# The first batch by halves of d with DMA transposes, and the seven-product form from the third chunk on

## The chip, the cores and the metric

One core of a Trainium2 chip runs the kernel. The metric is the device time of one execution in microseconds (us); lower is better.

## The reference

The input x has 8 batches of 3008 rows of 256 (f32). Each column d of a batch is convolved circularly with a filter, by a real FFT over the rows, a product with a complex filter, and the inverse FFT. The result goes through a two-layer MLP with 2048 hidden units and a leaky ReLU.

```python
X = np.fft.rfft(x, axis=1)
y = np.fft.irfft(X * (filt_r + 1j * filt_i)[None], n=x.shape[1], axis=1)
h = y.reshape(24064, 256) @ w_in          # w_in 256 x 2048
out = np.maximum(0.01 * h, h) @ w_out     # w_out 2048 x 256
```

## The kernel before

**The FFT.** 3008 = 94 x 32. A batch goes through four stages: s1 (matmuls with a 94-point DFT for each of 32 residues n), a transpose, s2 (32-point DFTs with twiddles, 24 groups of frequencies, then the product with the filter `fa_sb`), sa (the inverse 32-point DFTs), a second transpose, and sb (the inverse 94-point DFTs), whose results, 376 tokens for each of 8 groups h and each half dt of d, are copied to `yt`, the input of the MLP.

**The MLP** goes over 47 chunks of 512 tokens. `moe1` makes the hidden units of a chunk: 32 matmuls with 512 columns (L528) into two wide PSUM tiles, and eight leaky ReLUs on ACT (L531). The second layer of a chunk is done one chunk later. `plain` does it in 64 matmuls with 256 columns (L693). `products` does it in the Winograd form of Strassen's scheme: seven products of quarter matrices, 112 matmuls with 128 columns (L601), with four sums of the hidden units on VectorE (`act_sums`, L567) and sums of the results. Chunks with a number of at least `W0` = 3 take the second form. Its sums lie in `big0`.

**The order** of all instructions is written out. Every step is put on a heap with a time in units of which a chunk takes `SL` = 8, and issued in the order of these times; the numbers in `REST`, `PLANS`, `YD`, `AFTER`, `SUMS` and others are such times and delays. Batches 1 to 7 run their FFT between the chunks of the MLP. `REST` places six sb groups of batch 0 (`late_sb`) that are left over from the start.

**Batch 0** has a list of its own, `FIRST`: each word names a step, and each engine works through its own part in that order. `s1p`, `s2p`, `sap` and `sbp` are matmuls into one of the five banks b0 to b4; `s1e`, `sae`, `sbe` copy a bank to SBUF on ACT (A) or VectorE (D); `s2d` multiplies a bank with the filter on VectorE; `s2a` copies a bank to SBUF on ACT for `s2m` to multiply on GpSimd; `t1` and `t2` are VectorE's 32x32 transposes (L399, L445), four calls each; `x`, `w_out` issue loads; `xc` rounds the early part of x to f16; `warm` are matmuls without use; `blank` clears rows of `x_sb`. Steps with a first argument hf or dt work on a half of d.

**Loads.** SP's queue brings constants and the first `EARLY` = 6 of the 32 residues of x as f32 (L225). The rest of x, the tables f2 and i1, the filter (first the half hf = 0, then hf = 1) and the weights are cast to f16 by GpSimd's software queue (L207 to L238, L474). Batches 1 to 7 transpose with `dma_start_transpose` on SP after s1 (L277) and through DRAM after sa; batch 0 does not.

Of the kernel before, what the change touches and what calls it, by code (L numbers as in the profile page):

```python
# [78 lines left out]
def kernel(  # L79
# [210 lines left out]
    def paired(t):  # L290
        return t[:].rearrange("p (e n t) -> p n e t", n=Q, t=2)

    def spread(dst, n0, ps, copy, e0=0):
        nn, de = ps.shape[1], ps.shape[2] // 2
        copy(paired(dst)[:, ds(n0, nn), ds(e0, de)], ps.rearrange("p n (e t) -> p n e t", t=2))
# [528 lines left out]
```

## Time and profile before

| | |
|---|---|
| median of 3 runs | 740.85 us (740.0 to 741.22) |
| the profiled execution | 740.64 us, its span 738.8 us |
| TensorE, VectorE, ACT, GpSimd busy | 730.5, 508.7, 549.3, 168.0 us |
| TensorE's granted clock | 1.00 of full speed throughout |
| first matmul of the MLP (L528) | starts at 34.71 us |
| last matmul of the last product | ends at 734.85 us |

The span is what the profiler records of one execution; the execution's own time is somewhat longer. A line of a profile names the source line (L528), the engine (PE is TensorE, PEld its weight loads, DVE VectorE, ACT ScalarE, POOL GpSimd, SP SyncE; SPq, ACTq and POOLq their queues), the operation, the tiles it writes and reads, and how often; timelines begin with start and duration in us, and brackets give the engine's idle time before an instruction and what ended it.

### The profile page before, as it was taken

How to read it: one execution, taken by the hardware profiler on the slowest of the kernel's cores; microseconds unless marked ns; L12 is line 12 of the kernel's file. 1: busy time of each engine (PE TensorE's matmuls, PEld its weight loads, DVE VectorE, ACT ScalarE, POOL GpSimd, SP SyncE). 2: the span in 40 equal slices, each digit the busy share in tenths (PEclk: the TensorE clock that was granted, in tenths of full speed). 3: DMA queues.
4: the chain of work that ended last, by engine and by line, in shares of the span. 5: the costliest groups of instructions: out<-in, count | busy, mean ns of one | idle time of the engine just before them, and what ended most of it. 6: DMA issues, size and time to landing. Idle time of an engine off the chain costs nothing.

```text
span 738.8 us, 19530 instructions
## 1 busy us (share of the span) xinstructions
PE 730.5 (99%) x8129; PEld 521.8 (71%) x8129; DVE 508.7 (69%) x696; ACT 549.3 (74%) x763; POOL 168.0 (23%) x171
## 2 busy tenths in 40 slices
PE   8999999999999999999999999999999999999997
PEld 3666677777777777777777777777767777777776
DVE  7878557776677667676777668666767676465566
ACT  4775787887788778887688777888767777777762
POOL 5605411333221312212132322222031220000000
PEclk9999999999999999999999999999999999999999
DMA  9978778778755595556855477434863433112012
GB/s 203 228 109 171 189 150 170 178 172 167 188 134 126 138 193 143 130 145 126 183 131 137 122 157 169 115 90 110 149 172 95 117 106 94 55 55 66 29 46 71
DMA packets 128617, 98.44 MB, mean 133 GB/s; under 512 B 59296, under 2 KB 107296, under 8 KB 128336
## 3 DMA queue, kind: packets, MB, share of 16 engines
q1 hardware_dynamic: 112905, 79.37, 42.0%
q0 software_dynamic: 15056, 17.50, 15.7%
q8 instruction: 63, 1.03, 0.6%
q10 hardware_dynamic: 567, 0.32, 0.2%
q14 instruction: 26, 0.21, 0.1%
HBM read 45.97 MB, written 35.65 MB: 110 GB/s over the span
## 4 chain that ended last, share of the span: by engine, by line
PE 93%; SPq 2%; DMA 2%; DVE 1%; ACT 1%; POOL 0%; issue 0%; POOLq 0%
PE ph L528 42%; PE pf L601 18%; PE po_ps L601 18%; PE pf L269 2%; PE pf L362 2%; PE pf L315 2%; PE pf L337 2%; PE pf L693 1%; DMA x_sb<-in_x_dram 1%; PE po_ps L693 1%; SPq L277 1%; SPq L587 1%; DMA p_b_g<-p_b_g 1%; PE po_ps L384 0%; PE pf L436 0%; ACT yt L351 0%
## 5 line engine op out<-in xcount | busy, mean ns | idle before, releaser
L531 ACT ACTIVATE gt_c<-ph 128x1024 f16<-128x1024 f32 x376 | 385.4, 1025 | 132.3 <-PE ph L528 125.5
L528 PE MATMUL ph<-yt,w_in_sb 128*128 128x512 f16 x1504 | 447.3, 379 | 0.2 <-ACT yt L351 0.2
L601 PEld LDWEIGHTS <-gt_c 128*128 128x128 f16 x2800 | 201.8, 98 | 97.9 <-issue 1.3
L330 POOL TENSOR_TENSOR y_b_g<-p_b_g,p_b_g 128x512 f16<-128x512 f32 x84 | 118.1, 1407 | 421.1 <-DMA p_b_g<-p_b_g 288.1
L601 PEld LDWEIGHTS <-big 128*128 128x128 f16 x2128 | 151.4, 98 | 65.9
L528 PEld LDWEIGHTS <-w_in_sb 128*128 128x128 f16 x1504 | 117.7, 98 | 4.4 <-DVE yt L351 0.4
L324 DVE TENSOR_TENSOR p_b_g<-pf,fb_sb 128x512 f32<-128x512 f32 x78 | 53.7, 688 | 33.8 <-PE pf L315 20.3
L601 PE MATMUL po_ps<-wt_sb,gt_c 128*128 128x128 f16 x704 | 71.8, 219 | 0.0
L601 PE MATMUL pf<-wt_sb,gt_c 128*128 128x128 f16 x688 | 69.3, 219 | 0.0
L601 PE MATMUL pf<-wt_sb,big 128*128 128x128 f16 x704 | 68.7, 219 | 0.0
L601 PE MATMUL pf<-w_out_sb,gt_c 128*128 128x128 f16 x720 | 68.1, 219 | 0.0
L351 ACT CAST yt<-pf 128x376 f16<-128x376 f32 (+9 forms) x136 | 58.1, 441 | 12.2 <-PE pf L362 8.5
L601 PE MATMUL po_ps<-w_out_sb,gt_c 128*128 128x128 f16 x688 | 65.7, 219 | 0.0
L601 PE MATMUL po_ps<-wt_sb,big 128*128 128x128 f16 x688 | 65.5, 219 | 0.0
L567 DVE TENSOR_TENSOR gt_c<-gt_c 128x2048 f16<-128x2048 f16 x43 | 56.9, 1322 | 1.0
L327 DVE TENSOR_TENSOR p_b_g<-pf,fa_sb 128x512 f32<-128x512 f32 x84 | 57.2, 681 | 0.2
L567 DVE TENSOR_TENSOR big<-gt_c,big 128x2048 f16<-128x2048 f16 (+1 forms) x45 | 56.4, 1254 | 0.0
L567 DVE TENSOR_TENSOR big<-big,gt_c 128x2048 f16<-128x2048 f16 (+1 forms) x45 | 56.3, 1252 | 0.1
L567 DVE TENSOR_TENSOR big<-gt_c 128x2048 f16<-128x2048 f16 (+1 forms) x46 | 56.3, 1224 | 0.0
L339 ACT CAST big<-pf 128x512 f16<-128x512 f32 x84 | 49.0, 584 | 9.3 <-PE pf L337 7.4
L270 ACT CAST big<-pf 128x384 f16<-128x384 f32 x90 | 43.0, 479 | 11.5 <-PE pf L269 8.2
L362 PE MATMUL pf<-i_sb,big 128*128 128x94 f16 x448 | 37.0, 206 | 0.0
(98 smaller groups left out, 644.7 us busy)
## 6 DMA issues: line engine op xcount, KB each, us to landing
p_b_g<-p_b_g SPq DMA_DIRECT2D x156, 128.0 KB
out_dram<-ost_c_h SPq DMA_DIRECT2D x118, 128.0 KB
dz<-big SPq DMA_DIRECT2D x42, 256.0 KB
big<-dz SPq DMA_DIRECT2D x56, 192.0 KB
x_sb<-in_x_dram POOLq DMA_DIRECT2D x40, 192.0 KB, 4.2
x_sb<-in_x_dram POOLq DMA_DIRECT2D x2, 768.0 KB, 9.2
w_in_sb<-in_moe_w_in_dram POOLq DMA_DIRECT2D x1, 1024.0 KB, 13.1
w_out_sb<-in_moe_w_out_dram POOLq DMA_DIRECT2D x1, 1024.0 KB, 14.3
```

The source lines that it names most:

```text
L269: nc.tensor.matmul(ps[:, j, :], x_sb[:, 4 * h + j, ts(dt, P)], fwd1m[:, :NW], start=True, stop=True)
L270: copy(turn_in[:, :, dt, :, ds(4 * h, 4)], ps.rearrange("p n (q k) -> p k q n", q=4))
L324: nc.vector.tensor_tensor(p2[:], ps, fb, AL.mult)
L327: nc.vector.tensor_tensor(p1[:], ps, fa, AL.mult)
L330: ("y", b, g), lambda: nc.gpsimd.tensor_tensor(y1[:], p1[:], p3[:], AL.add)))
L339: nc.scalar.copy(st2[h % 3][:, ds(2 * (g % 2), 2), :], ps)
L351: copy(yt[:, dt, ds(to, 4 * n)].rearrange("p (a c) -> p a c", c=4), v[:, ds(a, n)])
L362: nc.tensor.matmul(ps[:, j, :], z2[h % 3][:, j, ts(dt, P)], i1_sb[:, 4 * h + j, :N1], start=True, stop=True)
L528: nc.tensor.matmul(ph[:, j, :], w_in_sb[:, dt, ts(ct, P)], yt[:, dt, ds(ci * CH % RING, CH)], start=(dt == 0), stop=(dt == NDT - 1))
L531: nc.scalar.activation(gts[ci][:, ds(2 * g, 2), :], ph, AF.Lrelu)
L567: nc.vector.tensor_tensor(*(v[:, ds(c0, n)] for v in (o, i0, i1)), op)
L601: nc.tensor.matmul(of[t], a()[:, c, ts(t, P)], w[:, c, :], start=(c == 0), stop=(c == NCH - 1))
```

## The change

In batch 0 the two halves of d go separate ways. The first half keeps VectorE's transposes after s1 (two calls), and its second transpose is done by four DMA transposes on SP (`turn2`); for that, its sa uses the products as weights. The second half takes x as weights in s1 and is transposed by three DMA transposes on SP (`turn1`), and keeps VectorE's second transposes (two calls). `FIRST` is a new list. Four more sb groups of batch 0 (first half of d, h = 4 to 7) leave it and are placed by `REST0` between the chunks. `EARLY` is 8, the rest of x comes in three loads of 8, `w_in` is loaded in two halves, and the first half of batch 1's x is issued earlier on GpSimd's queue. `W0` is 2, so that chunk 2 takes the seven-product form. The last stores of the last chunk use other queues, and many places and delays have new values.

```diff
@@ -99,29 +99,30 @@
     SL = 8
     NCH = NCT // 2
     QT = 4 * N1
-    W0 = 3
+    W0 = 2
     GAP = 0.6
     EXG = 0
     LANDED = 2.836
-    READ = 1.712
-    TURN = 0.889
-    TURNED = 2.3
-    TURNS = 1.015
-    MARGIN = 3.838
-    YD = (0.966, 1.75, 0.753, 0.432, 1.2)
-    SUMS_FIRST = (0.018, 2.103, 2.35, 4)
-    SUMS = (0.322, 1.569, 2.418, 4)
-    REST = (5.339, 14.69, 8.396, 11.015, 24.419, 20.72)
-    DUE = (3.52, 0.66)
+    READ = 1.863
+    TURN = 0.994
+    TURNED = 2.064
+    TURNS = 0.968
+    MARGIN = 3.703
+    YD = (0.966, 1.75, 0.753, 0.418, 1.2)
+    SUMS_FIRST = (0.01, 1.144, 2.226, 3.62)
+    SUMS = (0.322, 1.519, 2.723, 4)
+    REST = (5.723, 13.479, 13.889, 13.394, 25.953, 17.309)
+    REST0 = (0.946, 2.627, 7.4, 12.589)
+    DUE = (3.521, 0.66)
     TWICE = (2.2, 2.35)
     LEAD = (3.9, 7.293)
-    AFTER = (0.454, 0.757, 1.245, 2.615, 0.39, 0.731)
+    AFTER = (0.01, 0.757, 1.503, 2.615, 0.676, 0.653)
     PLANS = (
-        (0.01, 0.254, 12.6, 1.065, 4.3, 35.584, 2.78, 8.122, 1.518),
-        (23.983, 0.737, 42.87, 2.58, 7.4, 85.174, 2.85, 2.756, 2.12),
-        (47.4, 1.5, 77.28, 3.57, 5.62, 130.659, 2.547, 1.5, 1.552),
+        (0.141, 0.279, 12.6, 1.096, 4.948, 35.584, 2.78, 8.122, 1.518),
+        (23.983, 0.737, 42.87, 2.58, 7.4, 85.174, 3.091, 2.756, 2.12),
+        (47.008, 1.164, 77.28, 3.57, 5.62, 132.135, 2.547, 1.5, 1.552),
         (81.42, 2.0, 119.86, 3.87, 6.302, 177.538, 2.92, 1.5, 2.55),
     )
@@ -219,12 +220,12 @@
-    EARLY = 6
+    EARLY = 8
     x_early = big[1][:].bitcast(FP32)[:, : EARLY * D].rearrange("p (n d) -> p n d", n=EARLY)
     nc.sync.dma_start(small_sb[:, 0], small_d.ap()[:, 0])
     nc.sync.dma_start(x_early[:R1], bass.AP(tensor=x.tensor, offset=x.offset, ap=[[N2 * D, R1], [D, EARLY], [1, D]]))
     nc.sync.dma_start(small_sb[:, 1:], small_d.ap()[:, 1:])
-    for n0, nn in ((6, 10), (16, 10), (26, 6)):
+    for n0, nn in ((8, 8), (16, 8), (24, 8)):
         x_load(0, n0, nn)
     for i in range(2):
         nc.gpsimd.dma_start(f2_sb[:, ts(i, NC // FP), :], f2_d.ap()[i])
@@ -235,14 +236,22 @@
         if hf == 0:
             nc.gpsimd.dma_start(f2_sb[:, ts(2, NC // FP), :], f2_d.ap()[2])
     nc.gpsimd.dma_start(i1_sb[:], i1_d.ap())
-    nc.gpsimd.dma_start(w_in_sb[:], moe_w_in.rearrange("(dt p) c -> p dt c", p=P))
     nc.vector.memset(idle, 0.0)
...
-    nc.vector.memset(big[2][:].rearrange("p (e n t) -> p e n t", n=Q, t=2)[:, :, NC:Q, :], 0.0)
+    half = [t[:, ts(i, HALF)] for t in big for i in range(2)]
+    in0, in1, mid0, mid1, in2, in3 = half
+    mid1, in1 = (v[:, : NC * P] for v in (mid1, in1))
+    in1 = in1.rearrange("p (k q n) -> p k q n", k=NC, q=4)
+    mid1 = mid1.rearrange("p (k d) -> p k d", k=NC)
+    in2q = in2.rearrange("p (n q k) -> p n q k", n=N2, q=4)
+    out2 = in0.rearrange("p (n d) -> p n d", n=N2)
+    nc.vector.memset(big[1][R1:P, HALF + NC * P :], 0.0)
+    nc.vector.memset(in2q[:, :, :, NC:Q], 0.0)
+    nc.vector.memset(in3.rearrange("p (e n t) -> p e n t", n=Q, t=2)[:, :, NC:Q, :], 0.0)
     K4 = 4 * NC
...
@@ -384,33 +384,49 @@
             nc.tensor.matmul(po_ps.rearrange("p a d -> p (a d)"), idle[:, 0:P], idle,
                              start=True, stop=True)
-    def s1p(_, n0, n, b):
-        ps = fill(("s1", n0), b, n, D)
-        for j in range(0, n, 2):
-            nc.tensor.matmul(ps[:, ds(j, 2), :], fwd1[:N1], x_sb[:N1, ds(n0 + j, 2), :],
-                             start=True, stop=True)
-
-    def s1e(_, n0, n, e):
-        spread(big[0], n0, held.pop(("s1", n0)), engine[e])
+    def s1p(t, n0, b):
+        if t == 0:
+            ps = fill(("s1", t, n0), b, 4, DH)
+            nc.tensor.matmul(ps, fwd1[:N1], x_sb[:N1, ds(n0, 4), :DH], start=True, stop=True)
+            return
+        ps = fill(("s1", t, n0), b, 4, NW)
+        for j in range(4):
+            nc.tensor.matmul(ps[:, j, :], x_sb[:N1, n0 + j, DH:], fwd1m[:N1, :NW], start=True, stop=True)
+
+    def s1e(t, n0, e):
+        ps = held.pop(("s1", t, n0))
+        if t == 0:
+            engine[e](paired(in0)[:, ds(n0, 4)], ps.rearrange("p n (e t) -> p n e t", t=2))
+        else:
+            engine[e](in1[:, :, :, ds(n0, 4)], ps.rearrange("p n (q k) -> p k q n", q=4))
     def t1(i):
-        a = big[0][:].bitcast(FP32)[:, ts(i, E4 * Q)].rearrange("p (e n r) -> p e n r", n=Q // 2, r=2)
-        o = big[1][:].bitcast(FP32).rearrange("p (n e r) -> p e n r", n=Q // 2, r=2)
+        a = in0.bitcast(FP32)[:, ts(i, E4 * Q)].rearrange("p (e n r) -> p e n r", n=Q // 2, r=2)
+        o = mid0.bitcast(FP32).rearrange("p (n e r) -> p e n r", n=Q // 2, r=2)
         nc.vector.transpose(o[:, ts(i, E4)], a)
+    def turn1(c, n):
+        nc.sync.dma_start_transpose(mid1[:, ds(c, n)], in1[:, ds(c, n)].rearrange("p k q n -> p (k q n)"))
+
+    def turn2(h, n):
+        nc.sync.dma_start_transpose(out2[:, ds(h, n)], in2q[:, ds(h, n)].rearrange("p n q k -> p (n q k)"))
+
     def s2p(hf, c, n, i, b):
         ps = fill(("s2", hf, c, i), b, n, DH)
-        src = big[1][:].rearrange("p (n e r t) -> p n r e t", n=Q // 2, r=2, t=2)
+        src = mid0.rearrange("p (n e r t) -> p n r e t", n=Q // 2, r=2, t=2)
         for j in range(n):
-            v = src[:, (c + j) // 2, (c + j) % 2, ts(hf, DH // 2)]
+            v = mid1[:, c + j] if hf else src[:, (c + j) // 2, (c + j) % 2]
+            o = ps[:, j, :] if hf else ps[:, j, :].rearrange("p (e t) -> p e t", t=2)
             if i == 0:
-                nc.tensor.matmul(ps[:, j, :].rearrange("p (e t) -> p e t", t=2), f2_sb[:, c + j, :], v,
-                                 start=True, stop=True)
+                nc.tensor.matmul(o, f2_sb[:, c + j, :], v, start=True, stop=True)
                 continue
             for h in range(2):
-                nc.tensor.matmul(ps[ts(h, 64), j, :].rearrange("p (e t) -> p e t", t=2),
-                                 f2_sb[:, c + j, ts(1 - h, 64)], v, start=True, stop=True)
+                nc.tensor.matmul(o[ts(h, 64)], f2_sb[:, c + j, ts(1 - h, 64)], v, start=True, stop=True)
+
+    def load_w_in(i):
+        half = moe_w_in.shape[1] // 2
+        nc.gpsimd.dma_start(w_in_sb[:, :, ts(i, half)], moe_w_in.rearrange("(dt p) c -> p dt c", p=P)[:, :, ts(i, half)])
     def times_filter(eng, hf, c, n, i, x):
         eng.tensor_tensor(prods[hf][:, i, ds(c, n), :], x, fa_sb[:, ds(c, n), ts(hf, DH)], AL.mult)
@@ -432,25 +448,36 @@
     def sap(hf, c, b):
         ps = fill(("sa", hf, c), b, 4, DH)
+        if hf == 0:
+            for j in range(4):
+                for i, m in enumerate((inv2r, inv2i)):
+                    nc.tensor.matmul(ps[:, j, :], prods[0][:, i, c + j, :], m, start=(i == 0), stop=(i == 1))
+            return
         for i, m in enumerate((inv2r, inv2i)):
             nc.tensor.matmul(ps, m, prods[hf][:, i, ds(c, 4), :], start=(i == 0), stop=(i == 1))
     def sae(hf, c, e):
-        engine[e](paired(big[2])[:, ds(c, 4), ts(hf, DH // 2)],
-                  held.pop(("sa", hf, c)).rearrange("p n (t e) -> p n e t", t=2))
+        ps = held.pop(("sa", hf, c))
+        if hf == 0:
+            engine[e](in2q[:, :, :, ds(c, 4)].rearrange("p n q k -> p q n k"), ps.rearrange("p k (q n) -> p q n k", q=4))
+        else:
+            engine[e](paired(in3)[:, ds(c, 4)], ps.rearrange("p n (t e) -> p n e t", t=2))
     def t2(i):
-        a = big[2][:].bitcast(FP32)[:, ts(i, E4 * Q)].rearrange("p (e n r) -> p e n r", n=Q // 2, r=2)
-        o = big[0][:].bitcast(FP32).rearrange("p (h n e r) -> p h e n r", h=2, n=Q // 2, r=2)
-        nc.vector.transpose(o[:, i // 2, ts(i % 2, E4)], a)
+        a = in3.bitcast(FP32)[:, ts(i, E4 * Q)].rearrange("p (e n r) -> p e n r", n=Q // 2, r=2)
+        o = half[1].bitcast(FP32).rearrange("p (n e r) -> p e n r", n=Q // 2, r=2)
+        nc.vector.transpose(o[:, ts(i, E4)], a)
     def sb_matmuls(ps, dt, h):
         assert ("i1t",) not in issued
-        src = big[0][:].rearrange("p (h n e r t) -> p h n r t e", h=2, n=Q // 2, r=2, t=2)
+        src = half[1].rearrange("p (n e r t) -> p n r t e", n=Q // 2, r=2, t=2)
         for j in range(4):
             n2 = 4 * h + j
+            if dt == 0:
+                nc.tensor.matmul(ps[:, j, :], out2[:, n2], i1_sb[:, n2, :N1], start=True, stop=True)
+                continue
             for t in range(2):
-                nc.tensor.matmul(ps[64 * t : 64 * t + 64, j, :], src[:, dt, n2 // 2, n2 % 2, t, :],
+                nc.tensor.matmul(ps[64 * t : 64 * t + 64, j, :], src[:, n2 // 2, n2 % 2, t, :],
                                  i1_sb[:, n2, :N1], start=True, stop=True)
     def sbp(dt, h, b):
@@ -480,26 +507,26 @@
         nc.vector.memset(x_sb[R1:P, ts(i, N2 // 4), :], 0.0)
     FIRST = """
-        blank 0, blank 1, blank 2, xc 0 4 A, xc 4 2 D, blank 3, warm 18, s1p 0 0 4 b3, s1p 0 4 2 b0, warm 3, s1p 0 14 2 b1, s1e 0 4 2 D,
-        s1e 0 0 4 A, s1p 0 10 4 b4, s1e 0 10 4 A, s1p 0 6 4 b3, s1e 0 14 2 D, warm 4, s1p 0 20 4 b4,
-        s1e 0 6 4 D, s1p 0 16 4 b3, s1e 0 16 4 A, s1p 0 26 2 b2, s1p 0 24 2 b0, s1e 0 24 2 A, s1e 0 20 4 D,
-        s1p 0 28 2 b1, s1p 0 30 2 b4, s1e 0 26 2 D, s1e 0 30 2 A, s1e 0 28 2 D, t1 0, t1 1, warm 14,
-        s2p 0 0 4 0 b3, s2p 0 0 4 1 b2, warm 2, s2p 0 8 4 1 b0, s2a 0 0 4 0, s2a 0 0 4 1, t1 3,
-        s2p 0 12 4 1 b4, t1 2, s2d 0 8 4 1, s2p 0 12 4 0 b1, s2p 0 16 8 0 b3, s2m 0 0 4 0, s2m 0 0 4 1,
-        s2d 0 16 8 0, s2a 0 12 4 1, s2p 0 8 4 0 b2, s2p 1 16 8 0 b4, s2p 0 4 4 1 b0, s2a 0 12 4 0, s2d 0 8 4 0,
-        s2a 1 16 8 0, s2p 0 4 4 0 b1, s2p 1 16 8 1 b3, s2d 0 4 4 0, s2a 1 20 8 0, sap 0 8 b2, s2d 0 4 4 1,
-        s2a 1 16 8 1, s2a 1 20 8 1, s2m 0 12 4 0, s2p 0 16 8 1 b4, sap 0 0 b1, s2p 1 0 8 1 b3, s2m 0 12 4 1,
-        sap 0 12 b0, s2m 1 20 8 0, sae 0 8 A, s2d 0 16 8 1, sae 0 0 A, s2p 1 8 8 1 b4, sap 0 4 b2, s2d 1 0 8 1,
-        sap 0 16 b1, sae 0 12 A, s2p 1 8 8 0 b3, sap 0 20 b0, s2d 1 8 8 1, s2m 1 20 8 1, sae 0 4 A,
-        s2d 1 8 8 0, s2p 1 0 8 0 b4, sae 0 16 A, sap 1 20 b2, s2d 1 0 8 0, sap 1 12 b1, sae 0 20 A, sap 1 8 b0,
-        x 0, s2m 1 16 8 0, sae 1 20 A, s2m 1 16 8 1, x 1, w_out, sae 1 12 A, sae 1 8 A, sap 1 16 b3,
-        sae 1 16 A, sap 1 4 b2, t2 1, sae 1 4 A, sap 1 0 b4, t2 0, sae 1 0 A, warm 4, sbp 0 1 b1, sbp 0 4 b0,
-        sbp 0 0 b3, sbp 0 3 b2, t2 3, sbe 0 1 A, sbe 0 4 A, sbe 0 0 A, sbp 0 2 b4, sbp 0 7 b1, sbp 0 6 b0,
-        t2 2, sbe 0 2 A, sbe 0 7 A, sbp 0 5 b3, sbp 1 0 b4, sbp 1 1 b1, sbe 0 6 A, sbe 0 5 A, sbe 1 1 A,
-        sbe 0 3 D, sbe 1 0 D
+        blank 2, warm 14, blank 3, s1p 0 8 b2, blank 0, xc 4 4 D, blank 1, s1p 0 4 b4, xc 0 4 A, s1p 0 0 b3,
+        s1p 1 0 b0, s1e 0 4 A, s1p 1 4 b1, s1e 1 0 D, s1e 0 0 A, s1e 1 4 A, s1p 0 20 b4, s1p 1 8 b0, s1e 1 8 A,
+        s1p 0 12 b3, s1e 0 8 D, s1p 1 12 b1, s1p 0 16 b0, s1e 0 12 D, s1e 1 12 A, s1p 1 20 b1, s1p 0 28 b3,
+        w_in 0, s1e 0 16 A, s1p 0 24 b2, s1e 1 20 A, s1e 0 24 A, s1e 0 20 D, s1e 0 28 D, t1 1, s1p 1 16 b1,
+        s1p 1 24 b4, s1p 1 28 b2, warm 6, s1e 1 16 A, t1 0, s2p 0 0 8 0 b3, s1e 1 24 A, s1e 1 28 A,
+        s2p 0 0 8 1 b4, turn1 16 8, turn1 0 8, s2p 0 16 4 1 b1, s2p 0 16 4 0 b0, s2a 0 16 4 0, s2d 0 0 8 0,
+        s2a 0 16 4 1, s2p 0 8 8 0 b3, x 0, s2p 0 20 4 0 b2, s2d 0 0 8 1, s2p 0 20 4 1 b0, s2d 0 8 8 0,
+        s2a 0 20 4 0, s2p 0 8 8 1 b4, s2m 0 16 4 0, s2a 0 20 4 1, sap 0 0 b1, sap 0 4 b2, s2p 1 16 4 0 b0,
+        sae 0 0 A, s2d 0 8 8 1, s2p 1 0 8 0 b3, sap 0 8 b1, sae 0 4 A, s2p 1 0 8 1 b4, s2m 0 20 4 0,
+        s2a 1 16 4 0, s2d 1 0 8 0, turn1 8 8, s2p 1 16 4 1 b0, s2d 1 0 8 1, sae 0 8 A, s2m 0 16 4 1,
+        sap 0 12 b2, sap 0 16 b1, s2m 1 16 4 0, s2a 1 16 4 1, s2m 0 20 4 1, sae 0 12 A, s2p 1 8 8 0 b3,
+        sap 0 20 b2, sae 0 16 D, w_in 1, sae 0 20 A, s2d 1 8 8 0, s2p 1 20 4 0 b0, s2m 1 16 4 1, s2p 1 8 8 1 b4,
+        s2a 1 20 4 0, s2p 1 20 4 1 b1, sap 1 0 b2, s2d 1 8 8 1, sap 1 16 b3, sae 1 0 A, sap 1 4 b0, turn2 0 8,
+        sae 1 4 A, turn2 8 8, sap 1 12 b4, turn2 16 8, sap 1 8 b2, s2m 1 20 4 0, s2d 1 20 4 1, x 1, sae 1 12 A,
+        sae 1 16 D, sap 1 20 b1, turn2 24 8, sbp 0 0 b3, sae 1 8 D, sae 1 20 A, t2 1, sbe 0 0 A, warm 2, t2 0,
+        w_out, sbp 0 1 b3, sbe 0 1 D, sbp 0 2 b0, sbe 0 2 D, sbp 0 3 b2, sbp 1 0 b4, sbp 1 1 b1, sbe 0 3 A,
+        sbe 1 0 D, sbe 1 1 A
     """
-    steps = dict(s1p=s1p, s1e=s1e, t1=t1, s2p=s2p, s2d=s2d, s2a=s2a, s2m=s2m, sap=sap, sae=sae, t2=t2,
-                 sbp=sbp, sbe=sbe, x=load_x, w_out=load_w_out, xc=round_x, warm=keep_warm, blank=blank)
+    steps = dict(s1p=s1p, s1e=s1e, t1=t1, turn1=turn1, turn2=turn2, s2p=s2p, s2d=s2d, s2a=s2a, s2m=s2m, sap=sap, sae=sae, t2=t2,
+                 sbp=sbp, sbe=sbe, x=load_x, w_out=load_w_out, xc=round_x, w_in=load_w_in, warm=keep_warm, blank=blank)
     for step in FIRST.split(","):
         what, *args = step.split()
         steps[what](*(int(v) if v.isdigit() else v for v in args))
@@ -674,13 +701,13 @@  (last_three)
-            soon(0.02, lambda: (nc.sync, nc.scalar)[t].dma_start(*parts[0]))
+            soon(0.02, lambda: (nc.scalar, nc.sync)[t].dma_start(*parts[0]))
...
-            soon(0.02, lambda: store(ci, 2 + t, low[:, t, 1], P, P, queue=(nc.sync, nc.scalar)[t]))
+            soon(0.02, lambda: store(ci, 2 + t, low[:, t, 1], P, P, queue=nc.scalar))
@@ -702,6 +729,8 @@
     groups, first_use = [], {}
     for g in range(10, 16):
         at(REST[g - 10], lambda g=g: late_sb(1, g - 8, (act, dve)[g < 12 and g % 2]))
+    for h in range(4, 8):
+        at(REST0[h - 4], lambda h=h: late_sb(0, h, act))
     def plan(b, s1, s1_step, s2, s2_step, lag, sb, sb_step, xl, x_step):
         for g in range(16):
```

More of the change, by code (lines that the diff above doesn't have):

```diff
@@ L290, in paired @@
     def paired(t):
[L291 to L295, printed above, removed]
+        return t.rearrange("p (e n t) -> p n e t", n=Q, t=2)
     E4 = D // 2 // 4
-    def first_t1(i):
-        a = big[0][:].bitcast(FP32)[:, ts(i, E4 * Q)].rearrange("p (e n r) -> p e n r", n=Q // 2, r=2)
-        o = big[1][:].bitcast(FP32).rearrange("p (n e r) -> p e n r", n=Q // 2, r=2)
-        nc.vector.transpose(o[:, ts(i, E4)], a)
     ys = {}
@@ L396, in t1 @@
+    def s1e(t, n0, e):
[4 more added lines that the diff above has]
+            engine[e](in1[:, :, :, ds(n0, 4)], ps.rearrange("p n (q k) -> p k q n", q=4))
     def t1(i):
-        a = big[0][:].bitcast(FP32)[:, ts(i, E4 * Q)].rearrange("p (e n r) -> p e n r", n=Q // 2, r=2)
-        o = big[1][:].bitcast(FP32).rearrange("p (n e r) -> p e n r", n=Q // 2, r=2)
+        a = in0.bitcast(FP32)[:, ts(i, E4 * Q)].rearrange("p (e n r) -> p e n r", n=Q // 2, r=2)
+        o = mid0.bitcast(FP32).rearrange("p (n e r) -> p e n r", n=Q // 2, r=2)
```

## The prediction

> **What bounds the kernel now.** I read the page first, then the chain that ended last, the timeline of the first 45 us, the DMA tables of that stretch, and the waits of TensorE after it. The page and the chain say that TensorE sets the time once the MLP has started:
>
> ```profile
> PE 730.5 (99%) x8129; PEld 521.8 (71%) x8129; DVE 508.7 (69%) x696; ACT 549.3 (74%) x763; POOL 168.0 (23%) x171
> PE 93%; SPq 2%; DMA 2%; DVE 1%; ACT 1%; POOL 0%; issue 0%; POOLq 0%
> ```
>
> From the first L528 at 34.71 us to the last product at 734.85 the only wait of TensorE above 0.5 us that the waits give is one in batch 7, where a y block comes late:
>
> ```profile
> PE pf L337 <- POOL y_b_g L330: 1.2, 1, 1.2
> ```
>
> So the time is: when L528 can start, plus TensorE's dense work, plus few stalls, plus the tail (734.85 to 738.8). The change touches all four, the first most. The timeline of the start:
>
> ```profile
> 14.23 4.62 DVE L399 STREAM_TRANSPOSE big<-big 128x1024 f32<-128x1024 f32 x4
> 18.40 4.51 POOL L416 TENSOR_TENSOR prod<-spare,fa_sb 128x512 f16<-128x512 f32 x4 [0.25 <-DMA fa_sb<-in_filt_i_dram]
> 18.78 0.65 DVE L416 TENSOR_TENSOR prod<-pf,fa_sb 128x512 f16<-128x512 f32 x1
> 23.42 2.30 POOL L416 TENSOR_TENSOR prod<-spare,fa_sb 128x512 f16<-128x512 f32 x2 [0.50 <-DMA fa_sb<-in_filt_i_dram]
> 29.03 4.71 DVE L445 STREAM_TRANSPOSE big<-big 128x1024 f32<-128x1024 f32 x4
> 34.35 0.55 DVE L351 CAST yt<-ph 128x376 f16<-128x376 f32 x1 [0.17 <-ACT yt L351]
> 34.71 0.75 PE L528 MATMUL ph<-yt,w_in_sb 128*128 128x512 f16 x2 [0.22 <-ACT yt L351]
> ```
>
> Two things are to be seen. VectorE works almost without a gap from 18.78 to 34.90 (products with the filter, transposes, one copy), and the second L528 needs that copy. And the filter lands late: GpSimd waits for its first half until 18.38 (I call this F0) and for its second half until 23.40 (F1). Without L399's last two calls VectorE could not have multiplied before 18.38.
>
> The software queue that brings the filter is full there. Share of the 16 DMA engines (second last column; above 1 where packets overlap) and GB/s:
>
> ```profile
> 14.00:16.00 2.00, 2.00 (x11) 0.88 (x9) 1.85 (x3) 0.20 (x1) 1.26 (x3) 1.00 1.82 180
> 18.00:20.00 2.00, 1.65 (x33) 1.38 (x34) 1.44 (x3) 1.28 (x3) 1.75 (x3) 1.00 1.78 178
> 20.00:22.00 2.00, 2.00 (x40) 1.57 (x37) 2.00 (x3) 1.07 (x2) 2.00 (x3) 1.00 1.84 212
> ```
>
> **The change, part by part.** Terms are against the profiled execution (740.64 us, span 738.8), which lies 0.2 below the median of 740.85.
>
> *First half of d.* Two transposes instead of four stand before the first product with the filter. The last x lands at 12.31; one copy on ACT and one on DVE (0.66 each) follow, then two transposes of 1.16: VectorE is ready near 16.2 and TensorE's first s2p near 16.8 (16.71 now). But s2d needs F0. So VectorE idles until F0, and the 2.3 us that L399 gives up buy at most 18.78 - 18.38 = 0.4.
>
> *VectorE after F0.* In the new list it has four s2d of the first half, 4 x 1.22 = 4.9; then, needing F1, four s2d of the second half (4.9), one of 512 (0.68), three sae (3 x 0.66 = 2.0), two t2 (2.35) and three sbe (3 x 0.54 = 1.6): 11.5. Sum 16.4, against 16.1 now. The two transposes that go are given back as sae, as an sbe and a larger share of s2d. The end of the start is max(F0 + 4.9, F1) + 11.5; with the old F0 and F1 that is 23.4 + 11.5 = 34.9, just today's 34.90. Hence no gain, and each us by which F1 slips is a us lost.
>
> *What moves F1.* (1) Eight rows of x instead of six come as f32 by SP's queue. Both queues together move 223 GB/s into SBUF (below), so the 0.197 MB more of f32 cost 0.88 and the 0.098 MB less in the software queue save 0.44: +0.44 on all that follows; -0.44 if SP's queue were free.
>
> ```profile
> 4.00:6.00 2.00, 2.00 (x7) 0.77 (x6) 1.40 (x2) 0.00 (x0) 2.00 (x4) 1.00 1.06 223
> ```
>
> (2) Three DMA transposes (turn1) wait on SP for ACT's last s1e, near 15.1 to 15.9, and are issued back to back, 1.3 each as at L277. There they first move bytes 1.3 us after the issue began and move 128x1024 f16 (262 KB) at about 215 GB/s with the engines' share at 1, so 1.2 us of all engines:
>
> ```profile
> 48.96 1.36 SPq L277 DMA_TRANSPOSE big<-big  x1
> q1 hardware_dynamic: 595, 0.15, 37.0%
> ```
>
> (The second line is the DMA table from 48.9 to 51.0.) Thus 3.6 us of transposes begin at 16.4 to 17.2, before F0 and F1. What part of it delays the filter? A load of 192 KB of x beside one or two of them landed in 4.7 and 4.4 us instead of 4.2 and 4.3: 0.2 to 0.4 of 1.2 to 2.4, a part of 0.1 to 0.3. But that queue was nearly empty; two full queues (4 to 6 us) divided one rate, a part of 1. The nearest row in kind is the x load, in fullness the other; I take 0.4: 3.6 x 0.4 = +1.4, bounds +0.4 and +3.6.
>
> F1 = 23.4 + 0.44 + 1.4 = 25.3, and the start ends at 36.8: **+1.9** (bounds -0.4 and +4.1).
>
> The Trainium skill, "DMA: Bandwidth & Descriptors", section "Issuing engines are not separate DMA queues", says that DMAs of SP, ACT and GpSimd run on the same 16 engines and interleave, which speaks against this change; the 4 to 6 us row agrees. The same page ("DMA_TRANSPOSE effective BW") gives 261 GB/s, an estimate of 1.0 us for one transpose; by it the +1.9 would be +1.7.
>
> *Queues passed.* On GpSimd x 0 now stands before the first s2m: its issue (0.6) waits for a free slot. Today each software DMA issue from the ninth on waits for the landing of the one eight before, so x 0, the 17th, waits for F0 itself; s2m starts at F0 + 0.8. GpSimd then has 7 x 1.16 + issues, done before VectorE's sae 1 8: hidden. Half of w_in moves behind x 0, and x 1 and w_out keep their order. Today w_out lands at 43.4 and is first used at 45.30: 1.9 slack. With 7 transposes at the part 0.4 it lands 3.8 later, and the use is 1.9 + 1.2 (below) later: hidden, by 1.2; at part 1 it is not (rival). turn2 is hidden behind t2 if it lands by then; sbe 0 2 before sbe 1 0 is where it would show.
>
> *Four groups of the first d half (sb, h 4 to 7)* leave the start and come in chunks 0 and 1. On TensorE each is 4 matmuls of 94 columns, 0.17 (the L362 entries of the chain): +0.68. Three fall in chunk 0, where ACT is the bound: between 34.7 and 46 it is busy 10.6 of 11.3 us. Three more copies of 0.47 make +1.4, TensorE's 0.5 within it. I take **+1.2**, bounds +0.7 and +1.6.
>
> *Chunk 2 by seven products.* Plain: 64 matmuls at 0.109 = 6.98. Seven products: 112 at 0.0557 = 6.23.
>
> ```profile
> 49.02 0.44 PE po_ps L693 x4
> 727.64 0.89 PE po_ps L601 x16
> ```
>
> **-0.75**. VectorE's four sums (1.25 each) and larger adds come when batch 1's second stage has ended (place 24.7 of a 24 to 32 slot): hidden; without that cover up to +2.
>
> *Tail.* Today the last store waits on ACT's queue from 735.16 to 735.85 behind a 1.45 us issue. That one goes to SP, and ACT gets two issues of 0.6 instead: **-0.3** (0 to -0.4).
>
> *Places anew.* The wait of 1.2 in batch 7 arises where y's DMA stands behind transposes and stores on SP. Its order shifts by tenths of a slot, so it may go, stay or double: **-0.4** (-1.2 to +1).
>
> Sum: 1.9 + 1.2 - 0.75 - 0.3 - 0.4 = +1.65: profiled 742.3, median about 742.5.
>
> **The rivals.**
> 1. *Contention in full*: each transpose delays the software queue by all its 1.2 us. F1 = 23.4 + 0.44 + 3.6, start +4.1. w_out lands at 43.4 + 0.4 + 7 x 1.2 = 52.2, wanted at 45.3 + 4.1 + 1.2 = 50.6: 1.6 more. Total 4.1 + 1.6 + 1.2 - 1.45 = +5.4: 746. For: engines' share at 1.8. Against: the x loads. This is the rule of the Trainium skill named above, taken literally.
> 2. *Faster*: the transposes are hidden, as the x loads beside them nearly were, and F1 does not slip (-0.4), the copies moved to chunk 0 cost only TensorE's 0.7, the batch 7 wait goes (-1.2), product and tail give -0.75 and -0.4: -2.05, 738.7. It decides at F1 below 23.4; at 24.5 it is lost.
> 3. *No change*: hidden transposes, but ACT in chunk 0 takes the gain: about 740.5.
> 4. *A new wait in a later batch*: s2 groups are placed 2.064 instead of 2.3 after their transpose, 0.4 us closer in each of seven batches; if that was all the slack, up to +2.8 on the forecast: 745.
>
> **How the numbers follow.** A measurement tells about 0.2% (1.5 us) from no change. Chances: forecast 0.42 (its own range 741.0 to 744.5; 0.12 of it lies within 1.5 us), contention in full 0.22, faster 0.15, no change 0.14, new wait 0.07. Faster 0.15; same 0.12 + 0.14 = 0.26; slower 0.30 + 0.22 + 0.07 = 0.59. The range runs from rival 2's figure to just past rival 1's: 738.8 to 746.6.
>
> **What would show it.** Right: GpSimd's and VectorE's first L416 waiting for fa_sb after 18.4, and again at hf 1 near 25; VectorE idle from 16 to F0; the first L528 at 36 to 37; turn1's landing stretched beyond 3 us; ACT as releaser in chunk 0; 112 L601 more and 64 L693 fewer. Wrong: F1 at 23.4 or before, and L528 at 34 or earlier; or a start that ends later for another reason, such as turn2 landing after t2.

## The result, and the profile after

| | before | after |
|---|---|---|
| median | 740.85 us (740.0 to 741.57, 5 runs) | 782.71 us (781.02 to 784.87, 5 runs) |
| ratio | | 1.0571, 95% interval 1.0547 to 1.0596 |
| span of the profiled execution | 738.8 us | 780.9 us |
| first matmul of the MLP | 34.71 us (L528) | 71.28 us (L555) |
| last matmul of the last product | 734.85 us | 776.39 us |

The kernel is slower by 41.9 us. Slower was right; the size was not: 742.5 had been forecast, with 746.6 as the far end.

In the new source `moe1` is L555 (L528 before), the products L628 (L601), the filter's product on both engines L432 (L416), `s2p` L422, `sb` L477, `turn1` L409 and `turn2` L412. The page of after, first the busy times, then the chain's shares, the granted clock and the DMA share in 40 slices of 19.5 us:

```profile
PE 732.0 (94%) x8182; PEld 526.3 (67%) x8182; DVE 513.7 (66%) x702; ACT 547.9 (70%) x765; POOL 167.6 (21%) x171
...
PEclk8657999999999999999999999999999999999999
...
DMA  9999567688695568745595549634484432212112
...
PE 89%; DMA 8%; SPq 1%; issue 1%; ACT 1%; DVE 0%; POOL 0%; ACTq 0%; DVEq 0%; POOLq 0%
```

TensorE has the same work (732.0 against 730.5) in a span 42 us longer, and DMA has 8% of the chain instead of 2%. Most of what is out of order, the clock included, lies in the first four slices. The timeline of that stretch:

```profile
14.87 2.37 DVE L406 STREAM_TRANSPOSE big<-big 128x1024 f32<-128x1024 f32 x2 [0.35 <-ACT big L399]
...
16.01 24.65 SPq L409 DMA_TRANSPOSE big<-big  x3
...
18.47 4.62 DVE L432 TENSOR_TENSOR prod<-ph,fa_sb 128x1024 f16<-128x1024 f32 x4 [1.23 <-PE ph L422]
...
25.52 0.61 PE L422 MATMUL pf<-big,f_sb 128*128 128x128 f16 x4 [2.90 <-DMA big<-big]
...
40.49 2.26 POOL L432 TENSOR_TENSOR prod<-spare,fa_sb 128x512 f16<-128x512 f32 x2 [16.37 <-DMA fa_sb<-in_filt_i_dram]
...
49.75 1.04 PE L422 MATMUL ph<-big,f_sb 128*128 128x128 f16 x8 [23.62 <-DMA big<-big]
...
55.49 0.62 PE L422 MATMUL ph<-big,f_sb 128*128 128x128 f16 x8 [0.61 <-DMA big<-big]
...
69.77 0.81 PE L477 MATMUL pf<-i_sb,big 128*128 128x94 f16 x8 [8.11 <-DMA big<-big]
...
71.28 1.22 PE L555 MATMUL ph<-yt,w_in_sb 128*128 128x512 f16 x2
```

The first half of d runs nearly as forecast: VectorE is idle from 17.24 to 18.47, when both the filter's first half (F0; its last load, issued at 9.13, lands 9.2 us later, so still near 18.4) and the first s2p (17.72 to 18.44) are there. Then the three `turn1` transposes take 24.65 us to issue, where one takes 1.36 in a later batch, and TensorE waits for their data 2.90, 23.62 and 0.61 us, then 8.11 for `turn2`: 35.2 of the 36.6 us by which the MLP starts later. GpSimd's wait of 16.37 puts F1 at 40.5, against 23.4 before and 25.3 in the forecast.

The same stretch in windows of 5 us (busy us of TensorE, weight loads, VectorE, ACT, GpSimd; then granted clock, share of the DMA engines, GB/s):

```profile
20.00:25.00 5.00, 2.62 (x53) 2.24 (x50) 3.09 (x3) 3.13 (x6) 3.39 (x3) 0.97 1.63 173
...
30.00:35.00 5.00, 0.00 (x0) 0.00 (x0) 0.00 (x0) 0.00 (x0) 0.00 (x0) 0.50 1.31 136
...
45.00:50.00 5.00, 0.25 (x3) 0.26 (x4) 0.00 (x0) 0.00 (x0) 0.00 (x0) 0.50 1.07 33
```

No engine works from 30 to 35, and yet DMA packets are open all the time (a share of 1.31, and later 1.07), while what they move falls from 173 to 33 GB/s. The DMA tables (queue: packets, MB, share of 16 engines; q1 holds the transposes, q0 GpSimd's loads) tell the two phases apart. First 18 to 23, then 45 to 50:

```profile
q0 software_dynamic: 2531, 0.65, 127.7%
q1 hardware_dynamic: 896, 0.23, 34.4%
```

```profile
q1 hardware_dynamic: 243, 0.06, 95.2%
q0 software_dynamic: 31, 0.10, 12.0%
```

Until 23 GpSimd's packets have 256 bytes (0.65 MB in 2531), and a packet of the transposes takes 34.4% x 5 us x 16 / 896 = 31 ns. From 45 to 50 GpSimd's packets have 3 KB, and a 256-byte packet of the transposes takes 95.2% x 5 x 16 / 243 = 313 ns. In the kernel before, 48.9 to 51.0, the same division gave 37.0% x 2.1 x 16 / 595 = 21 ns. I call this the jam.

Of the 42.1 us of span, 36.6 lie ahead of L555, 5.0 between it and the last product (705.1 against 700.1), and 0.6 in the tail. In the middle, the largest piece is half clock: from 71.3 to 76.3 the granted clock is 0.54 after TensorE's idle time, which costs 5 x 0.46 = 2.3; the other pieces are waits from 95 to 100 and from 120 to 130, and one of 1.2 at 238.8, where an sb group waits for `dz`. The wait of 1.2 in batch 7 is down to 0.2.

### The profile page after: what moved, and what is told of

The parts are those of the page before. It is cut to its first block, busy times and chain, and to the rows that moved or that the text cites. A ratio compares the mean times of both kernels' runs of the same rounds, so it can differ in the third digit from the quotient of the medians.

```text
span 780.9 us, 19665 instructions
## 1 busy us (share of the span) xinstructions
PE 732.0 (94%) x8182; PEld 526.3 (67%) x8182; DVE 513.7 (66%) x702; ACT 547.9 (70%) x765; POOL 167.6 (21%) x171
## 3 DMA queue, kind: packets, MB, share of 16 engines
q8 instruction: 64, 1.05, 0.6%
## 4 chain that ended last, share of the span: by engine, by line
PE 89%; DMA 8%; SPq 1%; issue 1%; ACT 1%; DVE 0%; POOL 0%; ACTq 0%; DVEq 0%; POOLq 0%
PE ph L555 41%; PE po_ps L628 18%; PE pf L628 18%; DMA big<-big 6%; PE pf L362 2%; PE pf L315 2%; PE pf L337 2%; PE pf L278 2%; DMA x_sb<-in_x_dram 1%; PE pf L720 1%; PE po_ps L720 1%; SPq L409 1%; DMA big<-dz 0%; PE pf L480 0%; SPq L614 0%
## 5 line engine op out<-in xcount | busy, mean ns | idle before, releaser
L555 PE MATMUL ph<-yt,w_in_sb 128*128 128x512 f16 x1504 | 448.8, 380 | 0.0
L628 PEld LDWEIGHTS <-gt_c 128*128 128x128 f16 x2864 | 206.7, 98 | 100.3 <-issue 0.7
L628 PEld LDWEIGHTS <-big 128*128 128x128 f16 x2176 | 154.7, 98 | 67.8
L555 PEld LDWEIGHTS <-w_in_sb 128*128 128x128 f16 x1504 | 117.4, 98 | 4.6 <-issue 0.6
L351 ACT CAST yt<-pf 128x376 f16<-128x376 f32 (+7 forms) x137 | 58.8, 442 | 22.5 <-PE pf L362 9.6
L628 PE MATMUL pf<-wt_sb,gt_c 128*128 128x128 f16 x720 | 72.5, 219 | 0.0
L628 PE MATMUL po_ps<-wt_sb,gt_c 128*128 128x128 f16 x704 | 72.2, 219 | 0.0
L628 PE MATMUL po_ps<-w_out_sb,gt_c 128*128 128x128 f16 x752 | 71.4, 219 | 0.1
L628 PE MATMUL pf<-wt_sb,big 128*128 128x128 f16 x720 | 68.3, 219 | 0.0
L628 PE MATMUL po_ps<-wt_sb,big 128*128 128x128 f16 x704 | 67.8, 219 | 0.0
L628 PE MATMUL pf<-w_out_sb,gt_c 128*128 128x128 f16 x688 | 66.2, 219 | 0.0
L594 DVE TENSOR_TENSOR big<-big,gt_c 128x2048 f16<-128x2048 f16 (+1 forms) x46 | 60.0, 1304 | 0.1
L594 DVE TENSOR_TENSOR big<-gt_c 128x2048 f16<-128x2048 f16 (+1 forms) x47 | 58.9, 1254 | 0.0
L327 DVE TENSOR_TENSOR p_b_g<-pf,fa_sb 128x512 f32<-128x512 f32 x84 | 57.2, 680 | 0.2
```

The costliest lines, as they stand in the source:

```text
L327: nc.vector.tensor_tensor(p1[:], ps, fa, AL.mult)
L351: copy(yt[:, dt, ds(to, 4 * n)].rearrange("p (a c) -> p a c", c=4), v[:, ds(a, n)])
L555: nc.tensor.matmul(ph[:, j, :], w_in_sb[:, dt, ts(ct, P)], yt[:, dt, ds(ci * CH % RING, CH)], start=(dt == 0), stop=(dt == NDT - 1))
L594: nc.vector.tensor_tensor(*(v[:, ds(c0, n)] for v in (o, i0, i1)), op)
L628: nc.tensor.matmul(of[t], a()[:, c, ts(t, P)], w[:, c, :], start=(c == 0), stop=(c == NCH - 1))
```

## The experiments

Theory P: while transposes on SP and GpSimd's loads in large packets are in flight together, they hold each other up far beyond sharing. Rival S: whatever fills GpSimd's queue does that. Rival W: the new list and the new places are the cause, and the DMAs show it only. Kernels with one run are read by that run and its profile, beside one run of before on the same chip: 743.36 us for the three transposes alone, the plain copies and the loads moved, 739.86 for the small packets and for one turn undone at a time.

**Three transposes alone, early.** The kernel before, with three unneeded transposes into `wt_sb`, which is not yet in use, where `turn1` starts:

```diff
+    def extra(i):
+        nc.sync.dma_start_transpose(wt_sb[:, i], f2_sb[:, ds(8 * (i % 2), 8)].rearrange("p k d -> p (k d)"))
-        ... t1 0, t1 1, warm 14,
+        ... t1 0, t1 1, extra 0, extra 1, extra 2, warm 14,
```

> The kernel before plus three DMA transposes (262 KB each, from f2_sb into the still unused wt_sb) that nobody needs, issued on SP near 14.4 us, beside the small packets (256 B) of the filter. Theory P (a transpose's 256-byte packets and the LARGE packets of the software queue hold each other up; beside small packets they share): all three land by about 24, the filter's second half slips by 1 to 4 us, L528 starts at 36 to 39, 742 to 745 us. Theory S (a transpose beside any full software queue jams): the transposes take over 20 us in sum as in the changed kernel, L528 starts after 50, 756 us or more. Theory W (the transposes are harmless and the new order of loads and steps is the cause): 741, L528 at 34.7 to 35.5.

Measured: 750.38 us. The timeline:

```profile
13.12 8.59 SPq L480 DMA_TRANSPOSE wt_sb<-f_sb  x3
...
31.13 2.27 POOL L416 TENSOR_TENSOR prod<-spare,fa_sb 128x512 f16<-128x512 f32 x2 [8.38 <-DMA fa_sb<-in_filt_i_dram]
```

F1 goes from 23.40 to 31.13, by 2.6 us for each transpose: more than twice its own 1.2 and beyond the bound of 3.6 in all that the prediction had. The first matmul of the MLP starts at 43.11, and the time is 7.0 us above its before: both more than I had expected under P. Yet it is not the long jam: issue takes 8.59, not 24.65. The loads in flight here come in 256-byte packets.

**Three transposes alone, late.** The same, but reading `i1_sb`, and so issued at 26.5, when w_in, x and w_out are loading:

```diff
+        nc.sync.dma_start_transpose(wt_sb[:, i], i1_sb[:].rearrange("p n w -> p (n w)")[:, ts(i, 8 * P)])
```

> The same three extra transposes, but read from i1_sb, so that SP issues them when i1 has landed, near 25.7 us, beside w_in and the two halves of batch 1's x (large packets). Theory P: they jam, over 15 us from the first issue to the last landing, and w_in, x and w_out slip by as much; L528 or the first chunk waits, 750 to 770 us. Theory S: the same. Theory W: 741 to 743.

Measured: 754.6 us. Its timeline, TensorE's waits, and the DMA table from 30 to 35:

```profile
26.51 22.22 SPq L480 DMA_TRANSPOSE wt_sb<-i_sb  x3
```

```profile
PEld L269 <- DMA x_sb<-in_x_dram: 9.4, 1, 9.4
...
PEld L696 <- DMA w_out_sb<-in_moe_w_out_dram: 2.8, 1, 2.8
```

```profile
q0 software_dynamic: 24, 0.18, 172.6%
q1 hardware_dynamic: 524, 0.13, 17.8%
```

The jam, without the new list, the new layout or any user of the transposes: 22.22 us for three. Here it is GpSimd's side that stands: 172.6% x 5 x 16 / 24 = 5.8 us for a packet. From 32 to 39 next to nothing moves, 12 GB/s in all, and each queue passes 11 packets:

```profile
q0 software_dynamic: 11, 0.08, 6.1%
q1 hardware_dynamic: 11, 0.00, 0.3%
```

**Plain copies in their place.** The same bytes from the same tile at the same time, in 256-byte runs, not transposed:

```diff
+        nc.sync.dma_start(to[:, ds((0, 1, 16)[i], 8, step=2)], of[:, ds((0, 1, 8)[i], 8, step=2)])
```

> As the run before, but the three are plain copies of the same 262 KB in runs of 256 bytes instead of transposes. If small packets on SP's queue beside large packets of the software queue are enough for the jam: as the run with late transposes, 750 us or more. If it needs the transposing: the copies share the engines, under 4 us in sum each side, 741 to 744 us.

Measured: 744.24 us, 0.9 above its before. The same views:

```profile
27.02 11.04 SPq L482 DMA_DIRECT2D wt_sb<-i_sb  x3
```

```profile
q0 software_dynamic: 121, 0.85, 88.2%
q1 hardware_dynamic: 557, 0.14, 13.8%
```

GpSimd's packets take 88.2% x 5 x 16 / 121 = 0.58 us, a tenth of the time beside transposes, and five times as many pass. Small packets on SP's queue do not make the jam; transposing does.

**Small packets on the other side.** First a control: the kernel before, with w_in in four DMAs and each half of batch 1's x in two, all in 256-byte runs. Then the control with the three late transposes:

```diff
-    nc.gpsimd.dma_start(w_in_sb[:], moe_w_in.rearrange("(dt p) c -> p dt c", p=P))
+    for dt in range(NDT):
+        for odd in range(2):
+            nc.gpsimd.dma_start(w_in_sb[:, dt].rearrange("p (a c) -> p a c", c=P)[:, ds(odd, NCT // 2, step=2)],
+                                moe_w_in[ts(dt, P)].rearrange("p (a c) -> p a c", c=P)[:, ds(odd, NCT // 2, step=2)])
...
-        x_load(1, half * N2 // 2, N2 // 2)
+        for i in range(2):
+            x_load(1, half * N2 // 2, N2 // 2, i * DH, DH)
```

> The kernel before, with w_in (four DMAs) and both halves of batch 1's x (two DMAs each) loaded in runs of 256 bytes on the SBUF side, no extra transposes: the control for the next run. All theories: small runs move about 180 GB/s instead of 220, and GpSimd issues six DMAs more ahead of its products: 1 to 5 us slower than the kernel before, L528 at 35 to 38.

> The run before plus the three extra transposes issued when i1 has landed. Theory P (large packets of the software queue are what a transpose jams on): beside runs of 256 bytes the three need under 10 us from first to last issue, as the early ones did (8.6), instead of 22.2, and cost less than 6 us over the control. Theory S (any full software queue): 20 us or more of issue again, 10 us or more over the control.

Measured: the control 742.87, with transposes 748.85. Of the latter the timeline, TensorE's wait, and the table from 30 to 33, when the transposes are in flight:

```profile
25.61 6.77 SPq L484 DMA_TRANSPOSE wt_sb<-i_sb  x3
```

```profile
PE pf L272 <- DMA x_sb<-in_x_dram: 3.2, 2, 2.4
```

```profile
q1 hardware_dynamic: 1504, 0.38, 121.0%
q0 software_dynamic: 49, 0.01, 4.0%
```

The same loads with the same cast from f32 to f16, and the transposes are issued in 6.77 us instead of 22.22; a packet of theirs takes 121.0% x 3 x 16 / 1504 = 39 ns. S had foretold 20 us of issue or more and 10 us of cost, so it falls: a full queue is not enough for the long jam, its packets must be large. But the loads do not simply share here either: in these 3 us GpSimd's queue passes 49 packets, in the control 1728. The cost over the control, 6.0 us (one run each), is 2.0 us for each transpose, near the 2.3 of the early ones (7.0 / 3).

**The large loads moved out of `turn1`'s way.** The changed kernel, with i1, the first half of w_in and x 0 issued behind the fourth `s2m` on GpSimd:

```diff
-    nc.gpsimd.dma_start(i1_sb[:], i1_d.ap())
-        w_in 0, s1e 0 16 A, ...
-        ... s2p 0 8 8 0 b3, x 0, s2p 0 20 4 0 b2, ...
-        ... s2m 1 16 4 0, s2a 1 16 4 1, ...
+        ... s2m 1 16 4 0, i1, w_in 0, x 0, s2a 1 16 4 1, ...
```

> The changed kernel with the loads of i1, of the first half of w_in and of the first half of batch 1's x moved on GpSimd behind the fourth product (s2m 1 16 4 0), so that only small packets of the filter run beside turn1. Theory P: the three turn1 land by about 27 instead of 55, VectorE goes on by 28, the four turn2 still jam beside the moved loads (about 8 us); first L555 at 41 to 50 instead of 71, 750 to 762 us. Theory S: turn1 jams with the filter as before, L555 after 65, 775 us or more.

Measured: 766.7 us. The timeline and the waits:

```profile
15.91 9.35 SPq L408 DMA_TRANSPOSE big<-big  x3
...
33.61 20.87 SPq L411 DMA_TRANSPOSE big<-big  x4
```

```profile
PE ph L476 <- DMA big<-big: 13.3, 1, 13.3
...
PEld L421 <- DMA big<-big: 4.9, 2, 3.6
```

`turn1` now takes 9.35 us instead of 24.65, as P says. But the loads are then in flight beside `turn2`, whose four take 20.87 to issue; L557 starts at 55.84. I had not reckoned with so much. The time is 23.3 us above its before, against 41.9 for the changed kernel, a gain of 18.5; I had expected 750 to 762 us.

This slow `turn2` is not the standstill of the late experiment. The DMA table from 43 to 46:

```profile
q0 software_dynamic: 75, 0.58, 92.8%
q1 hardware_dynamic: 78, 0.02, 5.0%
```

A packet of the loads takes 92.8% x 3 x 16 / 75 = 0.59 us and one of the transposes 5.0% x 3 x 16 / 78 = 31 ns, as without a jam, and both queues together move 201 GB/s. But they pass almost the same number of packets, so 256 bytes of a transpose go with each 8 KB of a load, and the transposes crawl though nothing stands still. From 49 to 54, beside w_out's 512-byte packets, each queue passes 1204. So there are two effects: beside transposes the queues take turns by packets, whatever their size (beside the plain copies, 557 to 121, they did not), and in some stretches packets stand still besides.

**One turn undone at a time.** The changed kernel with `turn1` replaced by VectorE's transposes of the second half (`t1 3, t1 2`), and in another kernel `turn2` by those of the first half, each with the layout that belongs to it:

```diff
-        s2p 0 0 8 1 b4, turn1 16 8, turn1 0 8, ...
+        s2p 0 0 8 1 b4, t1 3, t1 2, ...
-        s2a 1 16 4 0, s2d 1 0 8 0, turn1 8 8, ...
+        s2a 1 16 4 0, s2d 1 0 8 0, ...
```

> The changed kernel with turn1 undone: the second half of d is transposed after s1 by two more VectorE calls, turn2 stays. If the transposes beside the software queue are the cause: the 35 us until L555 shrink by turn1's waits (24 to 27 us), while turn2 jams beside w_in, x and w_out for 8 to 20 us: L555 at 42 to 55, 748 to 762 us. If the new list or the order of loads is the cause: L555 stays above 62.

> The changed kernel with turn2 undone: the first half's second transpose is two more VectorE calls, turn1 stays. If the transposes are the cause: turn1 jams as before, last landing near 55, and only turn2's wait of 8 us goes: L555 at 60 to 66, 771 to 778 us. If turn2 was behind all of it: L555 below 45.

Measured: 779.84 without `turn1`, 768.79 without `turn2`. The timelines:

```profile
28.65 38.35 SPq L404 DMA_TRANSPOSE big<-big  x4
...
57.71 0.49 PE L469 MATMUL ph<-i_sb,big 128*128 128x94 f16 x4 [25.97 <-DMA big<-big]
```

```profile
15.24 15.90 SPq L409 DMA_TRANSPOSE big<-big  x3
...
43.84 1.03 PE L422 MATMUL ph<-big,f_sb 128*128 128x128 f16 x8 [20.05 <-DMA big<-big]
```

I had expected `turn1` to be the greater part (748 to 762 us without it, 771 to 778 without `turn2`). It is not so simple: either turn jams by itself, and without `turn1` the four of `turn2` meet w_in, both halves of x and w_out at once and take 38.35. L547, the first matmul of the MLP, then starts at 68.50; I had put anything above 62 down to the list, but the wait ahead of it is for `turn2`'s data. The costs do not add up: above their before the two take 40.0 and 28.9 us, so undoing one gains 1.9, the other 13 of the 41.9.

**Both undone.** The changed kernel with VectorE's transposes throughout, everything else as changed (5 rounds):

> The changed kernel with turn1 and turn2 both undone: all transposes of batch 0 by VectorE again (four calls t1, four t2), everything else of the change kept (list, EARLY 8, order of loads, late groups, chunk 2 in seven products, places, last stores). If the DMA transposes are the whole cause: F1 near 23.8, VectorE's work after F0 2.3 us longer than before, first L555 at 35 to 38, 741 to 746 us. If the new list or the loads cost tens of us by themselves: L555 after 45.

Measured: 750.19 us (746.01 to 751.38, 6 runs) against 741.18, ratio 1.0112 (1.0092 to 1.0133). VectorE's first four transposes end at 19.95 here; the prediction's list of 16.4 and two more transposes of 1.18 from there would end at 38.7. It ends at 37.88, and the MLP goes on from there:

```profile
37.22 0.39 PE L536 MATMUL ph<-yt,w_in_sb 128*128 128x512 f16 x1
...
37.94 0.39 PE L536 MATMUL ph<-yt,w_in_sb 128*128 128x512 f16 x1 [0.34 <-DVE yt L351]
```

```profile
85.00:90.00 5.00, 4.08 (x40) 2.46 (x38) 4.92 (x7) 3.55 (x6) 2.10 (x3) 1.00 0.74 145
90.00:95.00 5.00, 4.01 (x50) 2.95 (x49) 4.87 (x7) 3.11 (x4) 2.43 (x4) 1.00 0.91 231
```

So the seven transposes carry about 41.9 - 9.0 = 33 us of the 41.9, and W falls as the main cause. It keeps some 9 us in this kernel, more than I had expected (741 to 746). In the profiled execution (747.27) they are 2.5 at the start, about 1.9 from 85 to 95, where VectorE is full (the first seven-product chunk beside batch 1's second stage), and smaller waits. The rest goes with TensorE's clock: the six spans are 743.3 us at a mean granted clock of 0.999, 745.5 at 0.993 (the profiled one), and 748.1 to 749.6 at 0.990 or 0.991. In the profile the clock is at half from 10 to 20, where the kernel before has 1.00, so the new list loses it without any DMA transpose:

```profile
10.00:15.00 5.00, 4.28 (x11) 1.26 (x11) 3.10 (x5) 3.58 (x8) 2.44 (x4) 0.50 1.36 245
15.00:20.00 5.00, 5.00 (x31) 2.57 (x31) 4.65 (x6) 1.89 (x4) 2.80 (x5) 0.50 1.67 198
```

That the clock is the cause of the spread was not tried by itself.

**Chunk 2 alone, the tail alone, the places.** The kernel before with `W0 = 2`; with the two edits of the last stores; and with all the changed numbers (`W0`, `REST`, `PLANS`, `SUMS` and the others), but the old first batch and stores. 5 rounds each, against 741.18:

> The kernel before with W0 = 2 alone: chunk 2 in the seven-product form. 112 matmuls at 0.0557 instead of 64 at 0.109 us: -0.75 us, 739.5 to 740.6. If VectorE's four more sums make TensorE wait: 741 or more.

> The kernel before with the last stores on the changed kernel's queues alone. By my prediction's term: -0.3 us (0 to -0.4). By the changed kernel's profile, where the end lay 4.54 us after the last product instead of 3.95: +0.6 us, 741.2 to 741.8.

> The kernel before with all the changed kernel's numbers (W0 = 2, PLANS, REST, AFTER, SUMS, TURN and the others), but the old first batch and old last stores. -0.75 for chunk 2, and -1.2 if the wait of batch 7 goes without another in its place: 738.6 to 740.2. If the new places make a wait of their own, as the 1.2 us for z2 in the changed kernel near 239 us: 740 to 742.

| | median | ratio | 95% interval |
|---|---|---|---|
| `W0` = 2 | 742.33 us | 1.0014 | 1.0004 to 1.0025 |
| tail | 740.47 us | 0.9994 | 0.9984 to 1.0003 |
| all numbers | 743.21 us | 1.0027 | 1.0016 to 1.0038 |

Chunk 2 in seven products costs 1 us instead of bringing 0.75. Its windows, and its waits:

```profile
80.00:85.00 5.00, 4.44 (x41) 2.75 (x40) 4.07 (x7) 3.51 (x6) 2.25 (x3) 1.00 0.81 176
85.00:90.00 5.00, 4.51 (x44) 2.90 (x44) 3.87 (x5) 3.47 (x6) 2.98 (x3) 1.00 0.84 243
```

```profile
PE pf L269 <- DVE p_b_g L327: 0.8, 1, 0.8
```

TensorE is short of full by 1.05 us in ten; in the kernel before both windows are 5.00. The wait is for VectorE, which has batch 1's filter products (L327) still to do when the sums come. The tail makes no difference that can be told. The places as a whole make 2.0 us with `W0`, more than either range I had given, so about 0.9 of their own; the wait of 1.2 in batch 7 goes, but others come:

```profile
PE pf L270 <- DVE big L271: 1.0, 1, 1.0
...
PE pf L454 <- DVE p_b_g L328: 0.6, 1, 0.6
```

## Why the prediction was wrong, step by step

**F0 and VectorE's order: right.** F0 stayed at 18.4, and with both turns undone the list ended 0.8 before its reckoned place. VectorE's two transposes ended at 17.24, not 16.2, and the first s2p began at 17.72, not 16.8; that it cost nothing is owed to F0. The eight early rows of x, +0.44 on F1, fit too: with both turns undone F1 landed at 23.8 (issue at 16.01, landing 7.8 us later), 0.5 later than before.

**"What moves F1 (2)": the step that failed.** It took a part of 0.4 of each transpose's 1.2 us as delay, +1.4, with +3.6 as the end. Measured: F1 moved by 17.1, and `turn1` itself landed only by 55. Two things were wrong with it. The rate at which transposes delay even small packets is above 1, not 0.4: 2.6 us for each in the early experiment. So the bound that I called full contention, two queues that divide one rate, was no bound. The rows it rested on could not show it: the x loads that passed a transpose were few packets, and the two full queues at 4 to 6 us held no transpose. And beside large packets two things come on top that the sum did not have, the turns by packets and the standstill, for which no row of the kernel before existed, since it never has transposes and large loads from GpSimd in flight together during the start. The prediction reckoned `turn1`'s cost to others only, and not that it might itself be late, though it named "landing stretched beyond 3 us" as a sign.

The Trainium skill, "DMA: Bandwidth & Descriptors", section "Queues, rings and completion order", says that an engine takes its queues in turn, a packet at a time. The traces agree as to the count: 214 packets of the transposes and 213 of GpSimd's from 25 to 30 in the changed kernel, 1204 of each from 49 to 54 with the loads moved; the plain copies, 557 packets to 121, do not show it. By that rule a 256-byte packet of a transpose waits its turn behind packets of 3 to 8 KB, and that alone makes the transposes slow. But it would leave the two queues moving together about what they moved with the loads moved, 201 GB/s; they moved 137 and later 33 in the changed kernel and 12 in the late experiment. That part is the standstill. The same page's section "Rules for kernel authors" says that a transpose next to ordinary DMAs needs nothing; it says so where it warns of two transposing streams that spoil each other's data, and as to time, the runs here say otherwise.

**"turn2 is hidden behind t2 if it lands by then": wrong.** It landed 8.1 us late in the changed kernel, 26.0 late with `turn1` undone. **w_out and x hidden:** not tested where it was claimed, since the MLP itself began 36 us late; with three transposes alone they were late by 2.8 and 9.4.

**Rival 1** had the right cause in name and an eighth of the size (+5.4 of 41.9): it charged each transpose its own 1.2 us once. **Rivals 2 and 3** fall with F1. **Rival 4** asked for s2 groups that come too early for their data; the places gave about 0.9, mostly as waits for VectorE.

**Chunk 2**, -0.75, was +1: its cover (VectorE free when the sums come) was missing, and the price of that, up to +2, stood in the text. **Tail**, -0.3: nothing measurable. **Places**, -0.4: about +0.9. **Four late sb groups**, +1.2: not tested by themselves.

**Not in the sum at all:** the clock. After the long waits TensorE starts at half of it: the first two L555 took 1.22 us, the first two L528 of before 0.75. The Trainium skill, "TensorE: Matmul & The Clock Gate", section "What's actually happening", says that an idle TensorE falls to half its clock and needs some 3.4 us of work to come back. The windows agree as to the half (0.50 while idle and from 70 to 75); the return took longer here, since 0.91 from 75 to 80 puts it at 75.9, some 6 us after TensorE went back to work at 69.77. A first stretch at reduced clock came before any transpose: TensorE waited 3.01 us for x until 8.89, and the clock was 0.61 from 10 to 15 and 0.71 from 15 to 20, where the kernel before has 1.00 throughout.

**Open.** Why the packets stand still is not shown: the records do not say which packet waits for which. Nor is it shown how much of the 33 us is standstill and how much the turns by packets. Whether it must be GpSimd's queue, or any queue with large packets, was not tried, nor how it grows with the size of the packets (beside 256 bytes it is short, beside the 3 to 8 KB of w_in and x long). In the small-packet pair the number of DMAs changes too; the control holds that still.
